# Strassen's seven products for the second experts, and maxima over partitions without GpSimd

## The chip, the cores and the metric

The kernel runs on one core of one Trainium2 chip, in one launch. Its engines work side by side, each in its own order, and wait for one another by semaphores: PE (TensorE) multiplies, DVE (VectorE), ACT (ScalarE) and POOL (GpSimd) work element by element, SP (SyncE) issues the transfers. SBUF holds tiles, PSUM what the matmuls write. The metric is the device time of one execution in microseconds, the median of several runs.

## The reference

```python
attn = softmax(q @ k^T / 8 + bias, causal window of 128) @ v      # 4 batches, 8 heads, 576 positions, 64 wide
x = attn as 2304 tokens x 512
h = np.maximum(x @ w_in, 0.0); x = h * h @ w_out                  # 512 -> 2048 -> 512
logits = x @ w_gate; P = np.exp(logits - logits.max())            # 8 experts
for _ in range(8):
    P /= P.sum(1, keepdims=True) + 1e-09
    P /= P.sum(0, keepdims=True) + 1e-09
    P *= N / E
for e in range(8):
    h = np.maximum(x @ w1[e], 0.0)                                # 512 -> 1024
    out += P[:, e:e + 1] * (h @ w2[e])                            # 1024 -> 512
```

All inputs and the output are 32-bit floats.

## The kernel before

Each number that enters a matmul is split into two 16-bit floats, a high part (HI) and the remainder (LO). A product of two split numbers is three matmuls, `PAIRS`: high by high, high by low, low by high. The high part is made by ACT (`g_hi`, `ex_hi`), the low one by DVE, which subtracts the high part from the value (`g_lo`, `ex_lo`), or by POOL in the earlier parts (`minus`, L478).

The 2304 tokens are 18 tiles of 128, in five blocks j of 4, 2, 4, 4 and 4 tiles. The program has three parts that overlap at their edges: the attention (to about 430 us), the first experts (`h_part`, `y_part`, to about 600 us), and the second experts (from 594 us to the end), which the change rewrites.

In the second experts, for each expert e, each block j and each of 8 slices f of 128 hidden columns, `g_prod` (L1480) makes 12 matmuls with the weights as the stationary operand and the block's tokens as the moving one (512 columns, 256 in block 1) into one of two PSUM banks of tag h. ACT makes the ReLU's high part from PSUM (L1493), DVE its low part (L1497), and `o_prod` (L1506) multiplies each tile of 128 tokens by w2 into four banks of tag y, adding over f. At f = 7 `o_add` (L1523) adds each tile to the output's sum with the token's gate as factor. Each expert's weights are loaded by SP in eight pieces of 1024 columns; DVE takes each piece's largest magnitude (L1443), POOL the largest over the partitions (`all_max`, L256, an all-reduce), four small DVE steps make a power of two of it, and ACT and DVE split the pieces (L1461, L1467). The routing (`softmax_all`, `sink_all`, L1605) uses the same all-reduce on POOL. A maximum in the earlier parts is made in another way: DVE spreads the 128 partition values over a diagonal (`diagonal`, L269), PE multiplies a matrix of ones by it (`sum_all`, L264), and DVE takes the maximum along the row (`row_max`, L273).

The order in which each engine does its work is fixed when the program is built. The class `Plan` holds units (an engine, an assumed cost, what comes before, which buffers it takes and frees) and plays them through in assumed time; of the units that are ready on a free engine the one with the smallest rank goes first. What comes out is one order for each engine. On the chip an engine keeps to that order: an instruction that waits holds up all behind it on its engine. `GEMM` is the rank of work between matmuls, `LEAD2` how many slices `g_prod` is ahead of `o_prod`.

Of the kernel before, what the change touches and what calls it, by code (L numbers as in the profile page):

```python
# [15 lines left out]
MAXALL = bass_isa.ReduceOp.max  # L16
ADDALL = bass_isa.ReduceOp.add
# [125 lines left out]
def kernel(  # L143
# [66 lines left out]
    zeros = const.tile([P, P], F16, name="zeros")  # L210
# [44 lines left out]
    def all_max(dst, src):  # L255
        POOL.partition_all_reduce(dst, src, channels=P, reduce_op=MAXALL)  # L256

# [9 lines left out]
    def diagonal(src):  # L267
        t = small.tile([P, P], F32, tag="diag", bufs=2, name="diag")
        DVE.tensor_scalar(out=t, in0=ident, scalar1=src, scalar2=None, op0=ALU.mult)  # L269
        return t  # L270
# [10 lines left out]
    def make_zeros():  # L281
        DVE.memset(zeros, 0.0)
        DVE.memset(ones, 1.0)

    def keep_warm():
# [4 lines left out]
        for _ in range(2):  # L290
            PE.matmul(t, lhsT=zeros, rhs=zeros, start=True, stop=True)
# [22 lines left out]
    def make_tail():  # L314
# [11 lines left out]
            h=2, r=2, sq=4, y=4, stage=4, scr=1, hp=8, wst=4,  # L326
# [29 lines left out]
    TINY = 0.08  # L356

# [461 lines left out]
    def plan_own(i, n0, z, before):  # L819
# [5 lines left out]
        mx = unit(PE, 0.3, norms_sum, i, n0, rank=z, take=["s"], after=[constants["zeros"], *ns])  # L825
# [278 lines left out]
    def plan_weights(kind, g, z):  # L1104
# [11 lines left out]
        if kind == "in":  # L1116
# [3 lines left out]
            al = unit(PE, 0.45, w_sum, kind, g, rank=z, take=["s"], after=[dg[-1], constants["zeros"]])  # L1120
# [15 lines left out]
        if kind == "out":  # L1136
# [3 lines left out]
            al = unit(PE, 0.3, w_sum, kind, g, rank=z, take=["s"], after=[ad, constants["zeros"]])  # L1140
# [154 lines left out]
    def plan_block(j):  # L1295
# [76 lines left out]
        al = unit(PE, 0.45, y_sum, j, rank=GEMM, take=["s"], after=[dg, constants["zeros"]])  # L1372
# [17 lines left out]
    NP = KE // 2  # L1390
    SB = 2 * DM * 4
    NSLOT = 2 * NP
    assert SB == KD * 2 * P * 4 and NSLOT * 2 * SB <= 64 * 1024
    late = {}
    es = const.tile([P, E, 4], F32, name="es")
    eg = const.tile([P, 1], F32, name="eg")
# [5 lines left out]
    def open_late():  # L1402
        pool = ctx.enter_context(tc.tile_pool(name="late", bufs=1, side="right"))
        late["all"] = pool.tile([P, 2 * NSLOT * SB // 4], F32, tag="late", name="late")

    def piece_at(kind, n, dt=F16):
        return late_at((kind * NSLOT + n % NSLOT) * SB, SB, dt)

    def w1_slot(e, p):

        return piece_at(0, e * NP + p).rearrange("p (a k f c) -> p a k f c", a=2, k=KD, f=2)

    def w2_slot(e, p):

        return piece_at(1, e * NP + p).rearrange("p (a f d) -> p a f d", a=2, f=2)

    staged = {}

    def stage_of(e, kind, p):

        v = staged[e, kind, p]
# [4 lines left out]
    def ex_load(e, kind, p):  # L1426
# [378 lines left out]
```

## Time and profile before

| what | before |
|---|---|
| median of 3 runs | 2106.78 us (2104.64 to 2108.39) |
| the profiled execution, its own time | 2106.07 us |
| its span, first to last instruction | 2104.3 us |
| PE busy | 2011.2 us, 96% of the span, 11324 matmuls |
| DVE busy | 867.2 us, 41%, 1700 instructions |
| ACT busy | 578.5 us, 27%, 1188 instructions |
| POOL busy | 270.3 us, 13%, 270 instructions |
| mean granted clock of TensorE | 0.985 of 2.4 GHz |

Busy time of PE counts each matmul to its modelled end, and matmuls overlap: how long one costs in a stream is the distance between the starts of two, not its duration. For DVE, ACT and POOL the duration of an instruction runs into the start of the next by a little too. The arrow in a row of groups or of the timeline names what ended the idle time before an instruction.

### The profile page before, as it was taken

Reading aid. Unit: us, or ns where it says so; the run is one execution under the profiler, and the core shown is the slowest. Engines: PE = TensorE matmul, PEld = TensorE weight load, DVE = VectorE, ACT = ScalarE, POOL = GpSimd, SP = SyncE. Lnnn points to the kernel's source line nnn. Section 1 sums busy time; section 2 is a strip of 40 time slices with the busy share of each in tenths; the row PEclk is TensorE's granted clock in tenths of the full one; section 3 lists DMA queues with packets and bytes.
Section 4 is the critical chain, followed back from the end, with each engine's and each line's share of the span. In section 5 each row is a group of like instructions: output and inputs, shape, how many; then the busy total and the mean of one; then the engine's idle time right before and its main releaser. Section 6 shows DMA issues by size and latency. Waiting matters only on the chain.

```text
span 2104.3 us, 27282 instructions
## 1 busy us (share of the span) xinstructions
PE 2011.2 (96%) x11324; PEld 1025.9 (49%) x11324; DVE 867.2 (41%) x1700; ACT 578.5 (27%) x1188; POOL 270.3 (13%) x270
## 2 busy tenths in 40 slices
PE   8777878889999999999999999999999999999999
PEld 7744654444445444444544454454445445444544
DVE  5998988762265134125213422522342152211212
ACT  5766576532232222112111211211121121111110
POOL 2566555412200000000000000000000000000000
PEclk9999999999999999999999999999999999999999
DMA  7576788520030011002001100200110010000001
GB/s 194 139 184 115 128 152 145 98 88 1 1 99 23 1 40 41 1 11 70 1 1 31 51 1 1 81 1 1 31 50 1 1 41 1 1 1 1 31 21 40
DMA packets 209228, 100.61 MB, mean 48 GB/s; under 512 B 178128, under 2 KB 194512, under 8 KB 209104
## 3 DMA queue, kind: packets, MB, share of 16 engines
q1 hardware_dynamic: 209104, 98.87, 19.9%
q8 instruction: 88, 1.44, 0.3%
q14 instruction: 36, 0.29, 0.0%
HBM read 65.03 MB, written 4.72 MB: 33 GB/s over the span
## 4 chain that ended last, share of the span: by engine, by line
PE 79%; DVE 12%; issue 3%; ACT 2%; DMA 2%; POOL 1%; SPq 0%; DVEq 0%; POOLq 0%; ACTq 0%
PE o L1506 34%; PE g L1480 34%; PE h L1193 5%; PE y L1228 4%; DVE e L584 1%; DMA stage<-in_moe_w_dram 1%; ACT e L595 1%; DVE r L1208 1%; DVE bits_out L1065 1%; DVE kc L456 0%; PE s L569 0%; DVE r L1206 0%; DVE late L1467 0%; DMA eT<-eh 0%; DVE vo L456 0%
## 5 line engine op out<-in xcount | busy, mean ns | idle before, releaser
L1480 PE MATMUL g<-y,late 128*128 128x512 f16 (+1 forms) x3840 | 799.0, 358 | 3.1 <-DVE hp L1497 3.1
L1506 PE MATMUL o<-late,hp 128*128 128x512 f16 x3456 | 797.4, 379 | 0.0
L1497 DVE SCALAR_TENSOR_TENSOR hp<-g,hp 128x512 f16<-128x512 f32 (+1 forms) x320 | 203.5, 636 | 914.3 <-ACT hp L1493 914.2
L1480 PEld LDWEIGHTS <-late 128*128 128x128 f16 x3840 | 375.5, 98 | 388.8 <-issue 4.8
L1506 PEld LDWEIGHTS <-hp 128*128 128x128 f16 x3456 | 337.9, 98 | 394.1 <-issue 0.2
L1493 ACT ACTIVATE hp<-g 128x512 f16<-128x512 f32 (+1 forms) x320 | 177.1, 554 | 1191.1 <-PE g L1480 1191.0
L1228 PE MATMUL y<-sq,w_out 128*128 128x512 f16 (+2 forms) x1056 | 213.8, 350 | 14.7 <-POOL sq L478 9.9
L1193 PE MATMUL h<-xT,w_in 128*128 128x512 f16 (+2 forms) x1056 | 212.2, 349 | 6.2 <-ACT r L1200 4.2
L256 POOL PARTITION_ALL_REDUCE ema<-em x16 | 6.0, 375 | 1114.8 <-DVE em L1443 1099.4
L1228 PEld LDWEIGHTS <-w_out 128*128 128x128 f16 x1056 | 100.5, 102 | 97.2 <-issue 20.7
L1193 PEld LDWEIGHTS <-w_in 128*128 128x128 f16 x1056 | 99.4, 101 | 90.1 <-issue 12.0
L478 POOL TENSOR_TENSOR sq<-r,sq 128x512 f16<-128x512 f32 (+2 forms) x88 | 95.7, 1087 | 207.0 <-ACT sq L1213 190.8
L1206 DVE SCALAR_TENSOR_TENSOR r<-r,unit_s 128x512 f32<-128x512 f32 (+1 forms) x64 | 50.6, 792 | 100.5 <-ACT r L1200 100.4
L1467 DVE SCALAR_TENSOR_TENSOR late<-stage,es,late 128x1024 f16<-128x1024 f32 x56 | 70.7, 1281 | 17.1 <-ACT late L1461 17.1
L1443 DVE TENSOR_REDUCE em<-stage 128x1 f32<-128x1024 f32 x56 | 68.1, 1216 | 17.8 <-DMA stage<-in_moe_w_dram 17.4
L1200 ACT ACTIVATE r<-h 128x512 f32<-128x512 f32 (+2 forms) x88 | 44.8, 510 | 102.9 <-PE h L1193 96.2
L595 ACT ACTIVATE e<-e,nmax 128x256 f32<-128x256 f32 (+1 forms) x144 | 68.0, 474 | 17.1 <-DVE nmax L584 16.7
L1461 ACT ACTIVATE late<-stage,es 128x1024 f16<-128x1024 f32 x56 | 62.7, 1141 | 33.9 <-DVE es L253 24.2
L478 POOL TENSOR_TENSOR eh<-e,eh 128x512 f16<-128x512 f32 (+1 forms) x56 | 65.6, 1174 | 32.0 <-ACT eh L463 25.7
L1213 ACT ACTIVATE sq<-r 128x512 f16<-128x512 f32 (+2 forms) x88 | 48.4, 550 | 73.2 <-DVE r L1206 43.5
L1523 DVE SCALAR_TENSOR_TENSOR acc_wc<-o,pd,acc_wc 128x512 f32<-128x512 f32 x56 | 39.9, 744 | 54.1 <-PE o L1506 54.1
L1523 DVE SCALAR_TENSOR_TENSOR acc_wd<-o,pd,acc_wd 128x512 f32<-128x512 f32 x56 | 39.8, 743 | 36.3 <-PE o L1506 36.3
(193 smaller groups left out, 1157.3 us busy)
## 6 DMA issues: line engine op xcount, KB each, us to landing
stage<-in_moe_w_dram SPq DMA_DIRECT2D x56, 512.0 KB, 3.8
st_in<-in_moe_w_in_dram SPq DMA_DIRECT2D x16, 512.0 KB, 5.0
st_out<-in_moe_w_out_dram SPq DMA_DIRECT2D x16, 512.0 KB, 5.3
raw_k<-in_k_dram SPq DMA_DIRECT2D x17, 256.0 KB, 3.9
raw_v<-in_v_dram SPq DMA_DIRECT2D x17, 256.0 KB, 4.3
raw_q<-in_q_dram SPq DMA_DIRECT2D x16, 256.0 KB, 3.6
late<-in_moe_w_dram SPq DMA_DIRECT2D x8, 512.0 KB, 7.9
out_dram<-acc_wc SPq DMA_DIRECT2D x8, 256.0 KB, 2.1
```

The lines of the kernel that those rows point to most:

```text
L478: POOL.tensor_tensor(out=dst, in0=src, in1=hi, op=ALU.subtract)
L595: ACT.activation(out=e[:, n, c0:], in_=e[:, n, c0:], func=ACTF.Exp, scale=-1.0, bias=m["nmax"][:, h : h + 1], accum_out=m["sum"][:, h : h ...
L1193: PE.matmul(hp, lhsT=w[:, a, kk, r], rhs=xT[j][:, b, kk, c], start=(kk == 0 and a == b), stop=(kk == KD - 1 and a == LO),)
L1228: PE.matmul(hold["y", d][:, c], lhsT=w[:, a, f % FPC, d * P : (d + 1) * P], rhs=sq[:, b, c], start=(first and c.start == 0 and a == b), st ...
L1443: DVE.tensor_reduce(out=late["m", e, kind][:, p : p + 1], in_=staged[e, kind, p], op=ALU.max, axis=AX.X, apply_absolute_value=True,)
L1461: ACT.activation(out=w[:, HI], in_=stage_of(e, kind, p), func=ACTF.Copy, scale=es[:, e, 2 * kind + 1 : 2 * kind + 2])
L1467: DVE.scalar_tensor_tensor(out=w[:, LO], in0=stage_of(e, kind, p), scalar=es[:, e, 2 * kind + 1 : 2 * kind + 2], in1=w[:, HI], op0=ALU.mul ...
L1480: PE.matmul(pt, lhsT=w[:, a, kk, f % 2], rhs=homes[j][:, c, kk], start=(kk == 0 and a == c), stop=(kk == KD - 1 and a == LO),)
L1493: ACT.activation(out=t[:, HI], in_=hold["g", e, j, f], func=ACTF.Relu)
L1497: DVE.scalar_tensor_tensor(out=t[:, LO], in0=hold.pop(("g", e, j, f)), scalar=0.0, in1=t[:, HI], op0=ALU.max, op1=ALU.subtract)
L1506: PE.matmul(pt, lhsT=h[:, a, t * P : (t + 1) * P], rhs=w[:, c, f % 2], start=(f == 0 and a == c), stop=(f == KE - 1 and a == LO),)
L1523: DVE.scalar_tensor_tensor(out=A, in0=pt, scalar=pd[:, e, i : i + 1], in1=A, op0=ALU.mult, op1=ALU.add)
```

## The change

It touches the second experts, the weights that they read, and every maximum or sum over partitions that POOL made.

- Each product is cut into halves both ways: the hidden slices into pairs of 128 columns, the 512 inputs into two halves, the block's tokens into two halves (256 columns, 128 in block 1). Of the eight products of halves Strassen's form (Winograd's variant) leaves seven, of sums and differences of the halves. An expert is worked in two groups g, 16 in all; a group has two pairs p.
- `g_prod` is called seven times for a pair and block, each time with 6 matmuls of 256 columns (128 in block 1). They add up in three PSUM banks X, Z and Y. ACT copies what has to be kept (`g_copy`, three times), DVE adds the banks to the copies (`g_add`, three times), ACT takes the ReLU (`g_relu`, four times) into 32-bit floats in SBUF, POOL makes the four sums that the second product needs (`g_sum`), and ACT and DVE split seven results into high and low (`g_hi`, `g_lo`, seven times each). Before, ACT and DVE had one instruction each on 512 columns for a slice.
- `o_prod` is called seven times for a pair and block, each with 6 matmuls of 256 columns (3 in block 1); they add up over the group's two pairs in three banks, and each of the seven states of a bank is added to one quarter of the block's output by `o_add`, one instruction of 256 columns for each tile of tokens (in the first two groups one for the quarter).
- The same sums of the tokens (`t_minus`, `t_hi`, `t_lo`: T1 to T4) are made once, of the weights (`ex_sums` on POOL, then a second `ex_hi` and `ex_lo`) for each pair.
- The all-reduces on POOL become `diagonal`, `sum_all` and `row_max`, or `sum_all` alone for sums.

```diff
--- before.py
+++ after.py
-        POOL.partition_all_reduce(dst, src, channels=P, reduce_op=MAXALL)
...
+        late["m", g, kind] = sum_all(P, late["m", g, kind])
...
+            POOL.tensor_tensor(out=a22, in0=a22, in1=a21, op=ALU.add)
+            yield
+            minus(a21, a11, a21)
+            yield
+            minus(a11, a22, a11)
+            yield
+            minus(a12, a12, a11)
...
+    PROD = {
+        1: ("X", lambda kk: kk, (0, 0)),
+        2: ("Z", lambda kk: 2 + kk, (1, 0)),
+        5: ("Y", lambda kk: 11 + 2 * kk, "T1"),
+        6: ("X", lambda kk: 6 + 2 * kk, "T2"),
+        7: ("X", lambda kk: 7 + 2 * kk, "T3"),
+        4: ("X", lambda kk: 4 + kk, "T4"),
+        3: ("Y", lambda kk: 10 + 2 * kk, (1, 1)),
+    }
+    def bank(b, g, j, p):
+        if (b, g, j, p) not in hold:
+            tag, bufs = ("av", 1) if b == "Z" else ("h", 2)
+            hold[b, g, j, p] = ps.tile([P, cols[j]], F32, tag=tag, bufs=bufs, name=f"{b}{g}_{j}_{p}")
+        return hold[b, g, j, p]
+    def g_prod(g, j, p, x):
+        b, row, y = PROD[x]
+        w = w1_slot(g, p)
+        pt = bank(b, g, j, p)
+        for kk in range(KH):
             for a, c in PAIRS:
+                rhs = forms[j, y][:, c, kk] if isinstance(y, str) else quarter(j, c, *y)[:, kk]
                 PE.matmul(
-                    pt, lhsT=w[:, a, kk, f % 2], rhs=homes[j][:, c, kk], start=(kk == 0 and a == c),
-                    stop=(kk == KD - 1 and a == LO),
+                    pt, lhsT=w[:, a, row(kk), :], rhs=rhs, start=(x in (1, 2, 5) and kk == 0 and a == c),
+                    stop=(x in (2, 3, 4) and kk == KH - 1 and a == LO), skip_group_check=True,
                 )
...
-    def g_hi(e, j, f):
-        t = hold["hp", e, j, f] = hp_slot(j)
-        ACT.activation(out=t[:, HI], in_=hold["g", e, j, f], func=ACTF.Relu)
-
-    def g_lo(e, j, f):
-        t = hold["hp", e, j, f]
-        DVE.scalar_tensor_tensor(
-            out=t[:, LO], in0=hold.pop(("g", e, j, f)), scalar=0.0, in1=t[:, HI], op0=ALU.max, op1=ALU.subtract
-        )
-
-    def o_prod(e, j, f, t):
-        if f == 0:
-            hold["o", e, j, t] = ps.tile([P, DM], F32, tag="y", bufs=4, name=f"o{e}_{j}_{t}")
-        pt, h, w = hold["o", e, j, t], hold["hp", e, j, f], w2_slot(e, f // 2)
-        for a, c in PAIRS:
-            PE.matmul(
-                pt, lhsT=h[:, a, t * P : (t + 1) * P], rhs=w[:, c, f % 2], start=(f == 0 and a == c),
-                stop=(f == KE - 1 and a == LO),
-            )
-
...
+    def g_copy(g, j, p, x):
+        t = hold["t", x, g, j, p] = t_slot(j)
+        ACT.activation(out=t, in_=bank("Y" if x == "c" else "X", g, j, p), func=ACTF.Copy)
+    def g_add(g, j, p, x):
+        t = hold["t", x, g, j, p]
+        DVE.tensor_tensor(out=t, in0=bank({"a": "Z", "b": "Y", "c": "X"}[x], g, j, p), in1=t, op=ALU.add)
+    def g_relu(g, j, p, x):
+        if x in "abc":
+            t = src = hold["t", x, g, j, p]
+        else:
+            t, src = t_slot(j), bank(x, g, j, p)
+            hold["t", x, g, j, p] = t
+        ACT.activation(out=t, in_=src, func=ACTF.Relu)
+    PLACE = {"A11": "a", "A12": "X", "A22": "c", "S1": "c", "S3": "b", "S2": "a", "S4": "X"}
+    def g_sum(g, j, p, name):
+        a, b, c, X = (hold.get(("t", x, g, j, p)) for x in "abcX")
+        if name == "S1":
+            POOL.tensor_tensor(out=c, in0=c, in1=b, op=ALU.add)
+        elif name == "S3":
+            minus(b, b, a)
+        elif name == "S2":
+            minus(a, c, a)
+        else:
+            minus(X, X, a)
+    def g_hi(g, j, p, name):
+        f = hold["f", name, g, j, p] = hp_slot(j)
+        ACT.activation(out=f[:, HI], in_=hold["t", PLACE[name], g, j, p], func=ACTF.Copy)
+    def g_lo(g, j, p, name):
+        f = hold["f", name, g, j, p]
+        DVE.tensor_tensor(out=f[:, LO], in0=hold["t", PLACE[name], g, j, p], in1=f[:, HI], op=ALU.subtract)
+    OUT = {
+        1: ("X", "A11", 0, (0, 0)), 2: ("Z", "A12", 1, (0, 0)), 6: ("X", "S2", 6, (0, 1)), 5: ("Y", "S1", 3, (1, 1)),
+        7: ("X", "S3", 4, (1, 1)), 3: ("Y", "S4", 2, (0, 1)), 4: ("X", "A22", 5, (1, 0)),
+    }
...
+    def o_prod(g, j, p, x):
+        b, name, row, _ = OUT[x]
+        f, w, pt = hold.pop(("f", name, g, j, p)), w2_slot(g, p), o_bank(b, g, j)
+        for t in range(half[j]):
+            for a, c in PAIRS:
+                PE.matmul(
+                    pt[:, t], lhsT=f[:, a, t * P : (t + 1) * P], rhs=w[:, c, row],
+                    start=(x in (1, 2, 5) and p == t == 0 and a == c),
+                    stop=(x in (2, 3, 4) and p == NP - 1 and t == half[j] - 1 and a == LO),
+                    skip_group_check=True,
+                )
...
+            for t in range(n):
+                DVE.scalar_tensor_tensor(
+                    out=A[:, t], in0=pt[:, t], scalar=pd[:, g, i + t : i + t + 1], in1=A[:, t], op0=ALU.mult, op1=ALU.add
+                )
...
+        p1 = prod(1, 0, [*after, *prev], ["h"])
+        p2 = prod(2, 1, [p1], ["av"])
+        p5 = prod(5, 2, [p1], ["h"])
+        a_ = copy("a", p1)
+        a = add("a", a_, p2)
+        plan.free(p2, "av", a)
+        ra = relu("a", a)
+        la = split("A11", ra)
+        p6 = prod(6, 3, [a_])
+        b_ = copy("b", p6)
+        c_ = copy("c", p5)
+        p3 = prod(3, 4, [c_])
+        b = add("b", b_, p3)
+        plan.free(p5, "h", b)
+        rb = relu("b", b)
+        p7 = prod(7, 5, [b_])
+        c = add("c", p7, c_)
+        rc = relu("c", c)
+        lc = split("A22", rc)
+        p4 = prod(4, 6, [c])
+        rX = relu("X", p4, take=["t"])
+        plan.free(p1, "h", rX)
+        lX = split("A12", rX)
+        s1 = total("S1", rb, lc)
+        l1 = split("S1", s1)
+        s3 = total("S3", s1, ra)
+        l3 = split("S3", s3)
+        s2 = total("S2", s3, la)
+        l2 = split("S2", s2)
+        s4 = total("S4", s2, lX)
+        l4 = split("S4", s4)
```

In the order that the plan gives, three places show what moves.

DVE in the second experts, before: rows of the program before, in block 4 of expert 1. g is the PSUM bank of `g_prod`, hp the split result, stage the loaded weights, em the maximum, late the split weights.

```order
L1497 SCALAR_TENSOR_TENSOR hp_7065<-g1_4_4_9394,hp_7065 128x512
L1443 TENSOR_REDUCE em_9372<-stage_7026 128x1
L1497 SCALAR_TENSOR_TENSOR hp_7065<-g1_4_5_9423,hp_7065 128x512
L1467 SCALAR_TENSOR_TENSOR late_5981<-stage_7026,es_86,late_5981 128x1024
L1497 SCALAR_TENSOR_TENSOR hp_7065<-g1_4_6_9452,hp_7065 128x512
```

DVE in the second experts, after: rows of the changed program, where group 10 ends and group 11 begins. X, Y and Z are banks of the first product, oX and oY of the second, late and x1 the 32-bit results in SBUF, hp0 and hp1 the split ones, acc the output's sum.

```order
L1651 TENSOR_TENSOR hp1_7165<-late_5885,hp1_7165 128x256
L1651 TENSOR_TENSOR hp0_7164<-late_5885,hp0_7164 128x256
L1696 SCALAR_TENSOR_TENSOR acc_wd_7474<-oY10_3_21073,pd_90,acc_wd_7474 128x256 x2
L1620 TENSOR_TENSOR x1_7133<-Y11_0_0_21142,x1_7133 128x256
L1451 TENSOR_REDUCE em_20367<-stage_7082 128x1
L1620 TENSOR_TENSOR late_5885<-X11_0_0_21101,late_5885 128x256
L266 TENSOR_REDUCE ema_21217<-em_20367 128x1
L1696 SCALAR_TENSOR_TENSOR acc_wd_7474<-oX10_3_20950,pd_90,acc_wd_7474 128x256 x2
L262 TENSOR_SCALAR diag_21229<-ident_66,ema_21217 128x128
L1651 TENSOR_TENSOR hp1_7165<-late_5885,hp1_7165 128x256
```

Between two matrix products DVE had one instruction of the chain; now adds, low parts and output sums stand in one row, and the low parts (L1651) read both their operands from SBUF, where L1497 read one from PSUM.

POOL at the end of the first experts, before: sq is the low part for `y_part`, the rows without a tile belong to the all-reduce's lines.

```order
L478 TENSOR_TENSOR sq3_4_6056<-r3_4_0_5982,sq3_4_6056 128x512
L256 ISA
L256 ISA ema_6093<-em_6051 128x4
L478 ISA
L478 TENSOR_TENSOR sq3_5_6100<-r3_5_0_6082,sq3_5_6100 128x512
```

The same place after: late are the weights of group 0, summed by `ex_sums`.

```order
L471 TENSOR_TENSOR sq3_5_6068<-r3_5_0_6014,sq3_5_6068 128x512
L1500 TENSOR_TENSOR late_5885<-late_5885 128x2x128
L471 TENSOR_TENSOR late_5885<-late_5885 128x2x128
L1500 TENSOR_TENSOR late_5885<-late_5885 128x2x128
L471 TENSOR_TENSOR late_5885<-late_5885 128x2x128 x4
L471 TENSOR_TENSOR sq3_6_6168<-r3_6_0_6152,sq3_6_6168 128x512
```

The all-reduce and the rows around it are gone; in their place seven sums of weights stand between two low parts.

POOL in the second experts had one all-reduce for each set of weights and nothing else. After: L1637 begins the four sums of a pair, the L471 behind it are the other three.

```order
L1637 TENSOR_TENSOR late_5885<-late_5885 128x256
L471 TENSOR_TENSOR late_5885<-late_5885 128x256 x3
L1637 TENSOR_TENSOR x1_7133<-x1_7133,late_5885 128x256
L471 TENSOR_TENSOR late_5885<-late_5885,x1_7133 128x256
L471 TENSOR_TENSOR x1_7133<-x1_7133 128x256 x2
L1500 TENSOR_TENSOR stage_7082<-stage_7082 128x2x128
L471 TENSOR_TENSOR stage_7082<-stage_7082 128x2x128 x3
```

The four sums of a pair follow one another, and the sums of weights stand between two pairs.

## Rows read from the trace of the kernel before

**Rows 1.** The page's chain that ended last, by engine, shares of span.

```profile
PE 79%; DVE 12%; issue 3%; ACT 2%; DMA 2%; POOL 1%; SPq 0%; DVEq 0%; POOLq 0%; ACTq 0%
```

**Rows 2.** Windows, 594:2104: us, busy of PE, PEld, DVE, ACT, POOL, clock.

```profile
594.00:2104.00 1510.00, 1502.58 (x7366) 717.98 (x7364) 456.85 (x723) 260.99 (x417) 9.55 (x24) 1.00 0.07 23
```

**Rows 3.** Groups by form, PE: names xcount | busy us, mean ns | idle.

```profile
L1506 PE MATMUL o<-late,hp 128*128 128x512 f16 x3456 | 797.4, 379 | 0.0
L1480 PE MATMUL g<-y,late 128*128 128x512 f16 x3072 | 704.7, 379 | 2.0 <-DVE hp L1497 2.0
...
L1480 PE MATMUL g<-y,late 128*128 128x256 f16 x768 | 94.3, 273 | 1.1 <-DVE hp L1497 1.1
```

**Rows 4.** Timeline of PE, 637 us: start us, us, line, operation, xcount.

```profile
637.41 1.47 PE L1480 MATMUL g<-y,late 128*128 128x256 f16 x12
638.72 2.75 PE L1506 MATMUL o<-late,hp 128*128 128x512 f16 x12
641.31 1.47 PE L1480 MATMUL g<-y,late 128*128 128x256 f16 x12
```

**Rows 5.** Timeline of PE at 74 us, products 128 columns wide.

```profile
73.93 0.83 PE L1193 MATMUL h<-xT,w_in 128*128 128x128 f16 x12
```

**Rows 6.** Timeline of all engines, 464 to 479 us, an all-reduce on POOL.

```profile
465.01 0.39 POOL L256 PARTITION_ALL_REDUCE ema<-em  x1 [5.89 <-PE h L1193]
...
472.56 2.26 POOL L478 TENSOR_TENSOR sq<-r,sq 128x512 f16<-128x512 f32 x2 [7.16 <-issue]
...
473.75 4.85 PE L1228 MATMUL y<-sq,w_out 128*128 128x512 f16 x11 [9.24 <-POOL sq L478]
```

**Rows 7.** Timeline of PE at 616 us, a maximum's product with ones.

```profile
616.90 0.38 PE L264 MATMUL total<-diag,ones 128*128 128x128 f32 x2
617.12 4.05 PE L1480 MATMUL g<-y,late 128*128 128x512 f16 x18
```

**Rows 8.** Groups by form: DVE, then POOL and ACT at 256 columns.

```profile
L1467 DVE SCALAR_TENSOR_TENSOR late<-stage,es,late 128x1024 f16<-128x1024 f32 x56 | 70.7, 1281 | 17.1 <-ACT late L1461 17.1
L1443 DVE TENSOR_REDUCE em<-stage 128x1 f32<-128x1024 f32 x56 | 68.1, 1216 | 17.8 <-DMA stage<-in_moe_w_dram 17.4
...
L1497 DVE SCALAR_TENSOR_TENSOR hp<-g,hp 128x256 f16<-128x256 f32 x64 | 27.1, 423 | 138.9 <-ACT hp L1493 138.9
...
L478 POOL TENSOR_TENSOR eh<-e,eh 128x256 f16<-128x256 f32 x12 | 9.8, 815 | 5.4 <-ACT eh L463 4.0 <-POOL eh L478 0.9 <-PE y L1228 0.4
...
L1213 ACT ACTIVATE sq<-r 128x256 f16<-128x256 f32 x20 | 8.2, 412 | 10.2 <-DVE r L1206 7.4 <-DVE r L1208 1.4 <-PE y L1228 1.4
```

**Rows 9.** Source L1206: xcount, ns min/median/max, first and last start, forms.

```profile
L1206 DVE SCALAR_TENSOR_TENSOR r<-r,unit_s x64: 467/750/1642, 196.6 to 592.1; 128x512 f32<-128x512 f32 x48, 128x256 f32<-128x256 f32 x16
```

**Rows 10.** Source L456: xcount, ns min/median/max, first and last start, forms.

```profile
L456 DVE SCALAR_TENSOR_TENSOR vo<-raw_v,sc,vo x15: 736/1140/1642, 87.2 to 380.2; 128x512 f16<-128x512 f32 x15
```

**Rows 11.** Source L653: xcount, ns min/median/max, first and last start, forms.

```profile
L653 DVE TENSOR_TENSOR x<-av,r x18: 676/690/693, 28.7 to 423.6; 128x512 f32<-128x512 f32 x18
```

**Rows 12.** Timeline at the kernel's end, two DVE instructions back to back.

```profile
2097.80 1.41 DVE L1523 SCALAR_TENSOR_TENSOR acc_wd<-o,pd,acc_wd 128x512 f32<-128x512 f32 x2 [7.10 <-PE o L1506]
```

**Rows 13.** Timeline of all engines at 361 us, DVE beside POOL.

```profile
360.67 0.74 DVE L456 SCALAR_TENSOR_TENSOR kc<-raw_k,sc,kc 128x512 f16<-128x512 f32 x1
...
361.47 1.28 POOL L478 TENSOR_TENSOR qc<-raw_q,qc 128x512 f16<-128x512 f32 x1 [0.74 <-ACT qc L463]
...
361.66 1.64 DVE L456 SCALAR_TENSOR_TENSOR vo<-raw_v,sc,vo 128x512 f16<-128x512 f32 x1
```

**Rows 14.** Windows view, 100 to 400 us, columns as in the second group.

```profile
100.00:400.00 300.00, 244.04 (x2041) 148.25 (x2041) 262.06 (x641) 193.97 (x512) 175.62 (x158) 0.94 0.74 142
```

**Rows 15.** Timeline of all engines at 1000 us, a product handed on.

```profile
1000.66 2.75 PE L1506 MATMUL o<-late,hp 128*128 128x512 f16 x12
1000.92 0.60 ACT L1493 ACTIVATE hp<-g 128x512 f16<-128x512 f32 x1 [4.58 <-PE g L1480]
1001.55 0.69 DVE L1497 SCALAR_TENSOR_TENSOR hp<-g,hp 128x512 f16<-128x512 f32 x1 [3.85 <-ACT hp L1493]
```

More of the change, by code (lines that the diff above doesn't have):

```diff
@@ L1139, in plan_weights @@
             ad = unit(DVE, TINY, w_out_add, g, rank=z, after=sq)
[L1140 removed]
+            al = unit(PE, 0.3, w_sum, kind, g, rank=z, take=["s"], after=[ad, constants["ones"]])
             us = chain(
@@ L1691, in plan_experts @@
+            if kind and g < PARTS:
+                gated[g] = unit(DVE, 0.1, first_gate, g, rank=8000, after=[scales[g, 0], sc])
+        gated = {}
         weights(0, 0)
         weights(0, 1)
+        forms_, room, room2 = plan_forms(lgt, gone[NP:])
+        early = unit(SP, 0.0, t_early, rank=-10, take=["t"] * T_EARLY, lag=0.0)
+        plan.free(early, "t", *room)
         sums = {}
+        prev = []
         first_z = LATER + 100 * KF * NB
-        for e in range(E):
-            if e == 1:
+        for g in range(NG):
+            if g == PARTS:
@@ new lines, in plan_experts @@
+                at += 100 * NP + LAG2 - LEAD2
+                last = []
+                for k_, x in enumerate(OUT):
+                    b, name, _, (r, c) = OUT[x]
+                    for p in range(NP):
+                        new = p == 0 and b not in begun
+                        last = [
+                            unit(
+                                PE, c_pe(3 * half[j], HD), o_prod, g, j, p, x, rank=at + 14 * (NP * k_ + p),
+                                take=["y"] if new else [], after=[fs[p][name][1], *ready[1][g * NP + p], read.get(b), *last],
+                            )
+                        ]
+                        if new:
+                            begun[b] = last[0]
+                        outs[p].append(last[0])
+                        plan.free(fs[p][name][0], "hp", last[0])
+                    first = (j, r, c) not in sums
+                    w = half[j] * HD
+                    eng, cost = (ACT, c_act(w, 0.1)) if first else (DVE, c_dve(w, 1.17) + (0.11 if g >= PARTS and half[j] == 2 else 0.04))
+                    u = unit(
+                        eng, cost, o_add, g, j, x, first, rank=GEMM,
+                        after=[last[0], gated[g], *ended, *sums.get((j, r, c), [])],
+                    )
+                    read[b] = u
+                    sums[j, r, c] = [u]
@@ L1744 @@
+                for b in begun:
+                    plan.free(begun[b], "y", read[b])
+                for p in range(NP):
+                    used[1][g * NP + p] = outs[p]
+                if g == NG - 1:
+                    for t in range(nt):
+                        unit(SP, 0.8, o_out, j, t, rank=GEMM, after=[*sums[j, t // half[j], 0], *sums[j, t // half[j], 1]])
+            if g + 1 < NG:
+                weights(g + 1, 0)
+                weights(g + 1, 1)
     with tc.manual_schedule():
-        u = constants["zeros"] = unit(DVE, 0.3, make_zeros, rank=-3)
+        u = constants["ones"] = unit(DVE, 0.2, make_ones, rank=-3)
```

479 lines of the change are left out of this document (303 added, 176 removed).

## The prediction

> **What bounds the kernel now.** I read the chain of waits first, then a window over the second experts, then PE's groups by form, then the timeline. The chain that ended last runs over PE for 79% of the span [rows 1]: the reader is to see that no other engine has more than 12% of it. From 594 us to the end PE is busy for 1502.6 of 1510 us, DVE for 457, ACT for 261, POOL for 10, at a granted clock of 1.00, the 2.4 GHz level [rows 2]. So this part ends when PE has done its matmuls. PE's idle time ahead of them sums to about 3 us [rows 3]. What a matmul costs in the stream comes from starts: twelve of 256 columns run from 637.41 to 638.72, 109.2 ns each, and the twelve of 512 columns behind them to 641.31, 215.8 ns each [rows 4]. Twelve of 128 columns take 0.83 us to the end of the last; a lone one lasts about 0.22, so the other eleven starts are 55.5 ns apart [rows 5].
>
> **What the change takes from PE.** Before: 6528 matmuls of 512 columns (3072 and 3456) and 768 of 256 [rows 3], 6528 x 0.2158 + 768 x 0.1092 = 1492.6 us. After, counted in the program: 5376 of 256 columns and 1344 of 128 in the first product, 6048 of 256 in the second, 11424 x 0.1092 + 1344 x 0.0555 = 1322.1 us. That is 170.5 us less, nearly the eighth that seven products of eight save; halving the columns costs almost nothing by these rows. The Trainium skill speaks against this: "TensorE: Matmul & The Clock Gate", section "Back-to-back issue gap", gives about 81 ns for each matmul of 128 columns in a stream that loads weights for each one. Rows 5 are such a stream and show 55.5. By the page the 1344 narrow ones would cost 34 us more; I keep the row.
>
> **What else leaves or comes on PE.** At 465 us POOL makes an all-reduce of 0.39 us and then does nothing for 7.16 us that the profile could put down to any wait; PE waits 9.24 us for the low part behind it, and its next eleven matmuls take 4.85 us where 2.54 would do, at the lower clock [rows 6]. With no all-reduce left this goes: 12 us with the slow start. But seven sums of weights now stand ahead of the next low part on POOL, and 33 sums for the tokens, two in three as long as POOL's 1.28 us in [rows 13] or a little less, fall in the same stretch; I count 8 us gained, with 12 and a loss of 5 as ends. The maxima come to PE: 33 products with ones at 0.22 us [rows 7] and eight narrow ones, 8 us. The old waits of 3 us go. The first pair of all has few second products to fill the waits inside it, and in the last block the second products stand alone: for these two ends no row exists; between nothing and 16 us I take 8.
>
> With PE as the only limit the span would be 2104.3 - 170.5 - 8 + 8 - 3 + 8 = 1938.8 us.
>
> **DVE, ACT and POOL for one pair.** A pair on a full block has 84 matmuls, 9.17 us of PE; there are 128 such and 32 half ones, worth 144 full ones. DVE's instructions overlap their neighbours by 0.076 us: two of 743 ns end after 1.41 [rows 12]. DVE does three adds from PSUM and seven low parts, each near 0.423 - 0.08 = 0.34 us [rows 8], and seven output sums with a factor from memory at 0.467 - 0.08 = 0.39 [rows 9]: 3.4 + 2.7 = 6.1 us. The weights of a group cost four maxima of 1.22 - 0.08 and four low parts of 1.28 - 0.08 [rows 8], four more of three quarters' size in two pieces (1.05), and two chains of small steps, taken as 0.8 each: 15.1 us on nine pairs' worth, 1.7 us. Together 7.8 of 9.17 us: 85%, where DVE had 30% [rows 2]. ACT has 14 instructions of at most 0.41 us [rows 8] and its share of the weights, no more than DVE's 1.2 us of low parts: under 7 us. POOL has four sums and 16 more for a group's weights, at most 0.82 us each [rows 8]: 3.3 + 1.5, under 5 us. None of the three is the limit by its work alone.
>
> **What the low parts wait for.** One term is missing, and the trace shows it in another stage. At 361.66 us a DVE instruction with both operands in SBUF takes 1.64 us where its twin a microsecond before takes 0.74; a POOL instruction that began at 361.47 ends at 362.75, and DVE ends 0.55 us after it [rows 13]. Of 15 such instructions the median is 1140 and the longest 1642 ns against 736 at the least [rows 10], with POOL busy for 176 of 300 us [rows 14]. An add with an operand in PSUM never passes 693 ns in the same stretch [rows 11]. So DVE stands still until POOL's instruction ends, where both its operands lie in SBUF. All seven low parts of a pair are of this kind now; before, L1497 read PSUM. The mean loss there was 0.40 us on 512 columns at a POOL share of 0.58; for POOL instructions half as long 0.2 us, up to 0.3 while POOL runs without a pause. In a pair POOL runs its four sums in a row and the low parts of the first three fall into it: 3 x 0.3, and 0.05 for each of the other four, 1.1 us. The lower end is chance meeting alone, some 0.3 us. DVE then needs 8.1 to 8.9 of 9.17 us.
>
> That alone does not pass PE, but the orders are fixed. After the seventh product PE needs DVE's add before it may start the fourth of the same pair, and in the changed order one or two units of six matmuls (0.66 us each) stand between. The handing on takes 0.26 us from PE's last start to ACT, 0.03 from ACT's end to DVE [rows 15], and the add 0.42: about 0.7 us if DVE is free. So there is 0 to 0.6 us of room, and a low part held up by POOL, or one output sum of two instructions (0.8 us), ahead of the add on DVE goes through to PE. Behind the waiting product on PE stand the next pair's products and the second products, which would be ready. I take 0.4 us of PE's time for each pair, a good third of 1.1 us, since DVE's 15% of idle time takes up the rest; bounds are 0 and the whole 1.1. 144 x 0.4 = 58 us.
>
> **The sum.** 1938.8 + 57.6 = 1996.4 us of span; the profiled execution had 1.8 us around its span (2106.07 against 2104.3), which gives 1998. The median of the runs was 0.7 us above that execution, and I leave the number at 1998.
>
> **The rivals.**
> *The waits are taken up.* DVE's idle time and the units between the products cover all of it. For it: the PSUM waits of before were covered nearly always, 3 us in 320 products [rows 3]. Against it: DVE had 70% of its time free then. The time is 1938.8 + 1.8 = 1941 us.
> *The hop decides.* Every seventh product meets a busy DVE: 0.8 us of output sum or 1.2 us of weights ahead of the add, 0.9 us lost on PE for each pair. 144 x 0.9 = 130 us, 2070 us. For it speaks the room of 0 to 0.6 us, against it that the plan puts the fourth product where it assumes the add done.
> *DVE becomes the limit, and the kernel slower.* If nearly every low part meets POOL at its worst, 0.90 us on 512 columns (1642 - 740), half of it here, six of them cost 2.7 us: DVE needs 10.5 us for a pair, 1.3 more than PE, 144 x 1.31 = 189 us, 2129 us. It decides from 1.2 us above PE's time on, 2.55 us of such waits in a pair. For it: POOL and DVE are fed by the same results one after the other, so that they meet more often than by chance, as in rows 10. Against it: POOL rests for nearly half of a pair. The Trainium skill has the rule in "SBUF — State Buffer", section "SBUF: two separate sides": whichever of the two starts first has the shared ports for its whole instruction; rows 13 agree, with the end 0.55 us after POOL's.
>
> **How the numbers follow.** Forecast (1955 to 2045 us) 0.50; waits taken up (below 1955) 0.22; the hop (2045 to 2103) 0.13; DVE the limit 0.13; a time within 0.2% of before, which is about what the measurement tells from no change, 0.02. Faster 0.85, same 0.02, slower 0.13. The range reaches from 1938, the sum with PE as the only limit and the larger gain at 465 us, to 2095, which takes in most of the hop and leaves out DVE as the limit.
>
> **What would show it.** Right: the granted clock stays at 1.00 after 600 us, starts of 256-column matmuls are 109 ns apart inside a unit, the wait of 9 us at 465 us is gone, PE's idle time in the second experts is 30 to 90 us and most of it is ahead of the first products, released by DVE's adds (L1620); L1651 has a median near 0.41 us and a long tail to about 0.8, L1620 has none. Wrong: idle ahead of the second products, released by low parts or output sums; L1651 as short at the median as at the tail; a clock below 1.00; or matmuls of 256 columns that start more than 115 ns apart.

## The result and the profile after

The changed kernel takes 2050.6 us, median of 4 runs (2041.8 to 2055.7); the kernel before took 2106.4 us in the same job. The ratio is 0.973, interval 0.970 to 0.977. The time lies in the predicted range, 53 us above the forecast; it is 6 us past the forecast's own band (1955 to 2045 us), in the band of "the hop decides". The profiled execution took 2050.96 us with a span of 2048.7.

The chain that ended last, answering to [rows 1], first line by engine, second by line:

```profile
DVE 46%; PE 35%; POOL 6%; issue 6%; ACT 4%; DMA 2%; SPq 0%; POOLq 0%; DVEq 0%; ACTq 0%
DVE hp L1651 13%; PE X L1588 9%; PE oX L1670 7%; DVE late L1490 7%; PE Y L1588 3%; PE h L1186 3%; PE y L1221 3%; DVE acc_wc L1696 3%; DVE acc_wd L1696 3%; PE oY L1670 3%; DVE em L1451 2%; PE Z L1588 2%; DVE late L1620 2%; POOL late L471 2%; PE oZ L1670 2%
```

PE had 79%; now DVE has the largest share, and in it the low parts of the hidden quarters (L1651) and of the weights (L1490). The window over the second experts, columns as in [rows 2]:

```profile
604.00:2048.00 1444.00, 1363.21 (x12908) 1207.21 (x12906) 1343.24 (x3086) 893.28 (x2471) 694.52 (x895) 1.00 0.09 26
```

DVE is busy for 93% where it had 30%, POOL for 48% where it had 1%, at the clock of before. PE is no longer without pauses, and the waits of PE in this stretch say who ends them (us in all, times, longest):

```profile
PE X L1588 <- DVE late L1620: 35.0, 43, 2.5
PE X L1588 <- DVE x L1620: 21.0, 23, 2.2
PE X L1588 <- DVE ema L266: 10.1, 13, 1.1
```

They stand ahead of products into bank X, and most end with DVE's adds. All pauses of PE in this stretch sum to 77 us, inside the 30 to 90 that the prediction named. DVE's groups by form in this stretch, answering to [rows 8] (count | busy, mean ns | idle before):

```profile
L1651 DVE TENSOR_TENSOR hp<-late,hp 128x256 f16<-128x256 f32 x539 | 295.0, 560 | 15.4 <-ACT hp L1647 13.4
L1651 DVE TENSOR_TENSOR hp<-x,hp 128x256 f16<-128x256 f32 x357 | 199.1, 564 | 8.3 <-ACT hp L1647 6.8
...
L1620 DVE TENSOR_TENSOR late<-X,late 128x256 f32<-128x256 f32 x79 | 32.5, 411 | 3.5 <-PE X L1588 3.4
```

The add, with one operand in PSUM, keeps 0.41 us; the low part, of the same width with both in SBUF, has a mean of 0.56. Of the low parts of 256 columns six in ten stay below 0.45 us, and the others reach up to 1.35, where the prediction had a tail to about 0.8 (rows of both widths together: ns at the least, median and most):

```profile
L1651 DVE TENSOR_TENSOR hp<-late,hp x673: 269/414/1350, 616.7 to 2035.2; 128x256 f16<-128x256 f32 x132, 128x128 f16<-128x128 f32 x37
L1620 DVE TENSOR_TENSOR late<-X,late x101: 275/408/425, 622.5 to 2028.4; 128x256 f32<-128x256 f32 x79, 128x128 f32<-128x128 f32 x22
```

PE's stream itself is as predicted:

```profile
604.67 0.82 PE L1588 MATMUL X<-y,late 128*128 128x256 f16 x6
605.33 0.82 PE L1588 MATMUL Z<-y,late 128*128 128x256 f16 x6
...
1003.70 0.50 PE L1588 MATMUL X<-late 128*128 128x128 f16 x6
```

Six starts of 256 columns take 0.66 us, 109 ns each, and six of 128 end after 0.50, that is 56 ns each behind the lone 0.22 [rows 5].

The second experts' part is best told by one number: its length, from the first product into X to the end of the span, less the 1322.1 us of its matmuls. Here it is 2048.7 - 604.67 - 1322.1 = 121.9 us. The prediction had 88.5 for it: 57.6 of waits, 8 of maxima, 8 of ends, and 14.9 of logits and end that before had too. The other 18.9 us of the miss (604.67 instead of 585.8) lie ahead of it.

The stall at 465 us [rows 6] is gone; from 400 to 500 us PE is busy for 99.6 of 100. But two others stand on PE in the first 600 us, both ahead of a maximum's product:

```profile
143.96 2.33 PE L1221 MATMUL y<-sq,w_out 128*128 128x512 f16 x10 [0.35 <-POOL w_out L471]
157.50 0.76 PE L257 MATMUL total<-diag,ones 128*128 128x128 f32 x2 [11.21 <-DVE nmax L577]
...
524.00 2.75 PE L1186 MATMUL h<-xT,w_in 128*128 128x512 f16 x12
534.12 0.76 PE L257 MATMUL total<-diag,ones 128*128 128x128 f32 x2 [7.37 <-DVE diag L262]
```

In the first, DVE had the diagonal ready at 146.8, but the product's bank was freed only by DVE's last read of the scores (L577), which DVE reached at 157.3. In the second, DVE reached the maxima late, since it had stood in its fixed order ahead of token forms (start, length, and idle before with its releaser):

```profile
523.50 0.69 DVE L1562 TENSOR_TENSOR late<-late 128x512 f16<-128x512 f32 x1 [7.63 <-ACT late L1558]
...
527.81 0.97 DVE L1562 TENSOR_TENSOR late<-late 128x512 f16<-128x512 f32 x1 [2.96 <-ACT late L1558]
```

And one gain was not predicted. The kernel before began with a pause on POOL of 7.84 us that no wait explains; after, the same instruction follows at once. Before, then after:

```profile
0.72 0.21 POOL L294 MEMSET ident<- 128x128 f32 x1 [0.29 <-POOLq L1790]
8.77 0.28 POOL L295 TENSOR_SCALAR_AFFINE_SELECT ident<-ident 128x128 f32<-128x128 f32 x1 [7.84 <-issue]
```

```profile
0.73 0.20 POOL L286 MEMSET ident<- 128x128 f32 x1 [0.29 <-POOLq L2095]
1.01 0.29 POOL L287 TENSOR_SCALAR_AFFINE_SELECT ident<-ident 128x128 f32<-128x128 f32 x1
```

### The profile page after: what moved, and what is told of

It reads as the page before. It is cut to its first block, busy times and chain, and to the rows that moved or that the text cites. A ratio compares the mean times of both kernels' runs of the same rounds, so it can differ in the third digit from the quotient of the medians.

```text
span 2048.7 us, 44009 instructions
## 1 busy us (share of the span) xinstructions
PE 1879.3 (92%) x16840; PEld 1519.0 (74%) x16840; DVE 1769.6 (86%) x4086; ACT 1218.0 (59%) x3258; POOL 1015.2 (50%) x1191
## 4 chain that ended last, share of the span: by engine, by line
DVE 46%; PE 35%; POOL 6%; issue 6%; ACT 4%; DMA 2%; SPq 0%; POOLq 0%; DVEq 0%; ACTq 0%
DVE hp L1651 13%; PE X L1588 9%; PE oX L1670 7%; DVE late L1490 7%; PE Y L1588 3%; PE h L1186 3%; PE y L1221 3%; DVE acc_wc L1696 3%; DVE acc_wd L1696 3%; PE oY L1670 3%; DVE em L1451 2%; PE Z L1588 2%; DVE late L1620 2%; POOL late L471 2%; PE oZ L1670 2%
## 5 line engine op out<-in xcount | busy, mean ns | idle before, releaser
L1588 PEld LDWEIGHTS <-late 128*128 128x128 f16 x6720 | 617.8, 98 | 153.2 <-issue 85.7
L1670 PEld LDWEIGHTS <-hp 128*128 128x128 f16 x6048 | 585.0, 98 | 71.1 <-issue 6.4
L1670 PE MATMUL oX<-late,hp 128*128 128x256 f16 x3456 | 468.1, 273 | 4.0 <-DVE acc_wd L1696 3.8
L1651 DVE TENSOR_TENSOR hp<-late,hp 128x256 f16<-128x256 f32 (+1 forms) x673 | 349.6, 534 | 17.1 <-ACT hp L1647 14.8
L1647 ACT ACTIVATE hp<-late 128x256 f16<-128x256 f32 (+1 forms) x673 | 256.2, 390 | 68.4 <-POOL late L471 49.7
L1588 PE MATMUL Y<-y,late 128*128 128x256 f16 (+1 forms) x1920 | 242.7, 263 | 2.5 <-ACT late L1616 1.2
L1651 DVE TENSOR_TENSOR hp<-x,hp 128x256 f16<-128x256 f32 (+1 forms) x447 | 228.2, 519 | 8.3 <-ACT hp L1647 6.8
L1670 PE MATMUL oY<-late,hp 128*128 128x256 f16 x1728 | 233.6, 273 | 0.0
L1588 PE MATMUL X<-late 128*128 128x256 f16 (+1 forms) x1728 | 205.9, 256 | 27.4 <-DVE x L1620 10.1
L1647 ACT ACTIVATE hp<-x 128x256 f16<-128x256 f32 (+1 forms) x447 | 169.9, 389 | 53.8 <-POOL x L471 43.7
L471 POOL TENSOR_TENSOR stage<-stage 128x256 f32<-128x256 f32 x210 | 169.1, 806 | 61.2 <-DVE late L1490 51.1
L471 POOL TENSOR_TENSOR sq<-r,sq 128x512 f16<-128x512 f32 (+2 forms) x88 | 97.1, 1104 | 154.0 <-ACT sq L1206 144.4
L1490 DVE SCALAR_TENSOR_TENSOR late<-stage,es,late 128x512 f16<-128x512 f32 (+2 forms) x180 | 169.8, 969 | 2.1
L1486 ACT ACTIVATE late<-stage,es 128x512 f16<-128x512 f32 (+2 forms) x180 | 134.2, 784 | 39.2 <-POOL stage L471 35.0
```

What stands on the lines that cost most here:

```text
L471: POOL.tensor_tensor(out=dst, in0=src, in1=hi, op=ALU.subtract)
L1486: ACT.activation(out=hi, in_=t, func=ACTF.Copy, scale=es[:, g, 2 * kind + 1 : 2 * kind + 2])
L1490: DVE.scalar_tensor_tensor(out=lo, in0=t, scalar=es[:, g, 2 * kind + 1 : 2 * kind + 2], in1=hi, op0=ALU.mult, op1=ALU.subtract)
L1588: PE.matmul(pt, lhsT=w[:, a, row(kk), :], rhs=rhs, start=(x in (1, 2, 5) and kk == 0 and a == c), stop=(x in (2, 3, 4) and kk == KH - 1 an ...
L1647: ACT.activation(out=f[:, HI], in_=hold["t", PLACE[name], g, j, p], func=ACTF.Copy)
L1651: DVE.tensor_tensor(out=f[:, LO], in0=hold["t", PLACE[name], g, j, p], in1=f[:, HI], op=ALU.subtract)
```

## The experiments

Unless said otherwise each is the changed kernel with one edit; times are medians. "Beyond" is the length of the second experts less 1322.1 us, and "start" their first product, both from the trace: 121.9 and 604.67 us for the changed kernel.

**No sums on POOL.** The 640 sums of hidden quarters are left out.

```diff
     def g_sum(g, j, p, name):
+        if name:
+            return
```

> The changed kernel without POOL's sums between hidden quarters (the 640 instructions S1 to S4 are left out, so the low parts read unsummed values); order of everything else as before. Theory: DVE is full in the second experts because its low parts (both operands in SBUF) stand still beside POOL. L1651 falls from a mean of 0.56 to about 0.42 us on 256 columns, DVE has some 150 us less to do, PE's 107 us of waits fall to about 40, and the time to 1970-2000 us. Rival (the hop): PE waits for the way copy, add, fourth product in a fixed order, whatever a low part lasts: L1651 shorter, time 2035-2050 us. Rival (DVE's own work): L1651 stays at 0.52 us or more, time within 10 us of 2050.

1989.6 us (1986.3 to 1990.5), 61 less than the changed kernel; beyond 61.3, start 605.29. Its low parts, in their groups by form:

```profile
L1653 DVE TENSOR_TENSOR hp<-late,hp 128x256 f16<-128x256 f32 x539 | 231.0, 441 | 20.5 <-ACT hp L1649 20.1
L1653 DVE TENSOR_TENSOR hp<-x,hp 128x256 f16<-128x256 f32 x357 | 152.2, 433 | 13.3 <-ACT hp L1649 13.0
```

The low parts are short again, DVE is busy for 1217 us instead of 1343, and half of what was beyond is gone. So POOL's sums are what lengthens them. The run takes away more than that, since ACT and DVE no longer wait for the sums either. That DVE is simply full in the changed kernel was my theory, and the next runs test it.

**One low part twice.**

```diff
+        for _ in range(2 if name == "A11" else 1):
             DVE.tensor_tensor(out=f[:, LO], in0=hold["t", PLACE[name], ...
```

> The changed kernel with one of the seven low parts of each pair (A11) made twice on DVE: 160 more instructions, 75 us of DVE at the measured lengths (128 of 0.5, 32 of 0.35 us). Theory: DVE has no room left, so nearly all of it comes out at the end: 2105-2125 us. Rival (the hop in a fixed order, DVE idle for 5%): the second one falls in DVE's pauses: 2055-2075 us.

2103.0 us (2096.7 to 2106.9), 52 more, a little under the theory's range; beyond 175.3. DVE is busy for 1409 us from the start on, 66 more, and 53 of these come out at the end.

**One low part on POOL.** A11's low part runs on POOL and is planned there.

```diff
-            lo = unit(DVE, c_dve(n), g_lo, ...
+            eng, cost = (POOL, c_pool(n) + 0.08) if name == "A11" else (DVE, c_dve(n))
+            lo = unit(eng, cost, g_lo, ...
```

> The changed kernel with one of the seven low parts of a pair (A11) made by POOL instead of DVE. DVE loses 160 instructions, some 85 us at their measured lengths; POOL has 160 of 0.5 to 0.8 us more. Theory (the time follows what DVE has to do, with its standing still beside POOL; leaving out the sums took 61 us, one low part more cost 52): 2005-2025 us, L1651 still at 0.56 us. Rival (POOL's longer share holds up the six others as much as was gained, or the sums come late): 2045-2075 us.

2055.0 us, no gain: the theory missed, and the time is the rival's. DVE has 34 us less to do (1308) where 85 were expected; the low parts left to it last 0.575 us on 256 columns instead of 0.562, with POOL busy for 55% of the stretch. Beyond is 129. So the time does not follow DVE's work alone. The order had changed: in the program, the work that stands on PE between a pair's seventh and fourth product is 1.32 us on average instead of 1.62, worked out over its 160 pairs with 2400 columns to a microsecond.

**A low part's price in the plan.** Not one instruction differs, only the order from the second experts on. The plan took a low part for 0.34 us; the trace has 0.41 alone and 0.56 beside POOL.

```diff
-            lo = unit(DVE, c_dve(n), g_lo, ...
+            lo = unit(DVE, c_dve(n) + 0.14, g_lo, ...
```

> The changed kernel with one number of the plan changed: a low part of a pair is planned 0.14 us longer, at the length that the trace shows beside POOL; the instructions are the same, in another order from the second experts on. Theory (DVE is full): the order moves little, 2035-2052 us. Rival (the order is at fault, PE's fourth and first products stand where the plan wrongly takes DVE's add for done): PE's waits fall to half, 1990-2015 us.

1993.6 us (1992.0 to 1998.4), 57 less: the rival. Beyond is 69.7. Of PE's waits these are the largest:

```profile
PE X L1588 <- DVE late L1620: 8.4, 11, 1.8
PE X L1588 <- DVE x L1620: 6.3, 6, 2.4
```

Its low parts still last 0.55 us:

```profile
L1651 DVE TENSOR_TENSOR hp<-late,hp 128x256 f16<-128x256 f32 x525 | 280.1, 549 | 9.2 <-ACT hp L1647 8.6
L1651 DVE TENSOR_TENSOR hp<-x,hp 128x256 f16<-128x256 f32 x371 | 201.1, 548 | 5.9 <-ACT hp L1647 5.4
```

DVE is busy for 1323 of 1392 us, 95%. What fell is the waiting of the two engines for each other: from the last start of the seventh product to the start of DVE's add the median is 1.01 us instead of 1.71 (in [rows 15] the next engine begins 0.26 us behind PE's last start). The plan in its own assumed time has 0.83 us there with the new price and had 0.60 with the old one. So with the old price DVE came 1.1 us later than planned, and with the new one 0.2. The work on PE between the seventh and fourth product grew too, from 1.62 to 1.73 us.

**The sums on DVE.** `g_sum` issues on DVE, planned there.

```diff
-        return unit(POOL, c_pool(n) + 0.08, g_sum, ...
+        return unit(DVE, c_dve(n), g_sum, ...
```

> The changed kernel with the sums between hidden quarters on DVE instead of POOL, planned there. DVE gets 640 instructions more, some 196 us undisturbed, and loses the standing still of about 120 us that the run without the sums showed. Theory (low parts stand still beside POOL): L1651 at 0.41-0.44 us, DVE at 97% or more, 2080-2115 us. Rival (a low part is long for another reason, as its two SBUF operands themselves): L1651 stays at 0.52 us or more, 2160 us or more.

2035.5 us (2026.6 to 2037.2), better than either side had. L1651 falls to means of 0.45 and 0.46 us with POOL busy for 231 of 1428 us, and DVE for 1401 us, 98%. Here DVE is full. The sums take 232 us on DVE, counted from each start to the next, and its busy time grows by 58 only: the low parts of the pairs alone are 135 us shorter in all.

**Short sums for the tokens.** 20 instead of 50 POOL instructions; the sums lack the low halves.

```diff
             minus(t, quarter(j, HI, *one), v)
             yield
-            POOL.tensor_tensor(out=t, in0=quarter(j, LO, *one), in1=t, op=ALU.add)
...
             minus(t, quarter(j, HI, *one), quarter(j, HI, *two))
             yield
-            minus(u, quarter(j, LO, *one), quarter(j, LO, *two))
             yield
-            POOL.tensor_tensor(out=t, in0=t, in1=u, op=ALU.add)
```

> The changed kernel with one POOL instruction instead of two or three for each of the tokens' sums (20 instead of 50 in all, the values are not the sums). Theory: the wait of 7.4 us on PE at 527-534 us comes from DVE, which stands behind low parts of token sums that POOL has not made yet; it goes, the second experts start at 596-599 instead of 604.7 us, the time is 2041-2045 us. Rival: it comes from the one bank and the one diagonal tile that all maxima share now: no change, 2048-2053 us.

2036.5 us (2030.9 to 2037.9), 14 less and more than expected; start 589.8 (runs with all the sums: 596.4 to 605.3), and from 500 to 605 us PE is busy for 104.4 us instead of 97.6 of 105. PE has no pause left from 500 us to the start. The token sums are the cause of the second stall.

**The maxima alone.** The kernel before, with its 25 all-reduces as products with ones.

```diff
-            al = unit(POOL, 0.4, ex_all, e, kind, rank=z, after=mx)
+            dg = chain(DVE, [TINY, 0.2], ex_diagonal, e, kind, rank=z, after=mx, lag=1.0)
+            al = unit(PE, 0.3, ex_all, e, kind, rank=z, take=["s"], after=dg[-1:])
```

> The kernel before, with one part of the change alone: the experts' maxima, the routing's maximum and its sums are products with ones, and nothing is an all-reduce on POOL. Theory: the wait of 9.24 us at 465 us and its slow start go and nothing else moves, 10 to 12 us less than before, 2093-2097 us. Rival: the products wait for DVE's diagonals and PE's stream is cut 20 to 30 times instead: 2102-2110 us.

2086.1 us, 19.6 less than before (ratio 0.991, 0.990 to 0.993), better than either side expected. PE's busy time from 0 to 100 us rises from 80.5 to 88.5 us and from 400 to 500 from 90.1 to 100.0: both pauses of POOL are gone, the one at the start too. Start 571.73.

**The first memset's price.** The change had replaced a memset planned at 0.3 us by one planned at 0.2. This puts the number back.

```diff
-        u = constants["ones"] = unit(DVE, 0.2, make_ones, rank=-3)
+        u = constants["ones"] = unit(DVE, 0.3, make_ones, rank=-3)
```

> The changed kernel with one number of the plan changed: the first memset is planned with 0.3 us, as in the kernel before, instead of 0.2; no instruction is another, but the order up to the logits is that of the kernel before. Theory: the 11.2 us for which PE stands at 146-157 us ahead of a total come from the other order alone, and go; the second experts start at 588-594 instead of 604.7 us, the time is 2032-2042 us. Rival (the attention part is slower for the granted clock or for the one diagonal tile, not the order): 2046-2055 us.

2034.4 us (2033.6 to 2035.5), 16 less, as the theory had it; start 589.23. With 0.3 the order on PE is that of before, row by row, up to the logits; with 0.2 it parts from it after the attention's first 18 units on PE. Six runs with 0.2 and an unchanged first part start their second experts at 596.4 to 605.3 us, mean 600.2, three with 0.3 at 588.6 to 589.2: 11.2 us apart. That this is also the length of the first stall is chance, since the stall does not go: the same product now waits 6.98 us, for another step of DVE, as it waited 6.61 us in the kernel before.

```profile
153.18 0.80 PE L257 MATMUL total<-diag,ones 128*128 128x128 f32 x2 [6.98 <-DVE diag L262]
```

The rest is other waits, and the clock: from 250 to 300 us the granted clock is 0.73 in all six with 0.2, and 0.86 to 0.90 in those with 0.3 and in the kernel before. Which waits are worth how much was not taken apart.

**Both numbers of the plan.**

> The changed kernel with the two numbers of the plan together: low parts of a pair 0.14 us dearer, the first memset at 0.3 us. Theory (two separate losses, 57 us in the second experts' order and 16 us in the attention part's): they add up, 1973-1983 us. Rival (the early gain is taken back later, since DVE is the limit behind it): 1988-1996 us.

1980.1 us (1978.2 to 1981.5): the gains add up, start 588.64, beyond 69.0. In the second experts the order on PE is that of the run with the low part's price alone, which had 69.7, as the run with the memset's price alone has the changed kernel's and 122.0 where that had 121.9. So the same order gives the same length within 1 us.

**All prices.** Both numbers, and these:

```diff
-        return chain(POOL, [c_pool(KH * cols[j])] * n, t_minus, ...)[-1]
+        return chain(POOL, [c_pool(KH * cols[j]) + 0.3] * n, t_minus, ..., lag=SLOW)[-1]
...
-        us = [unit(DVE, c_dve(n1, 1.17), ex_lo, ...
+        us = [unit(DVE, c_dve(n1, 1.17) + 0.3, ex_lo, ...
-        us.append(unit(DVE, c_dve(W, 1.17), ex_lo, ...
+        us.append(unit(DVE, c_dve(W, 1.17) + 0.2, ex_lo, ...
```

> As the one with two numbers, and the other work that meets POOL is planned at the length that the trace shows: the weights' low parts 0.3 and 0.2 us dearer, a POOL instruction of the tokens' sums 0.3 us dearer, and their result counted as there 1 us later. Theory (what is planned too short comes late, and the engine behind it stands): the wait of 7.4 us at 527-534 us goes and some of the waits in the second experts, 1958-1972 us. Rival (what is left is DVE's own work): 1973-1983 us as without it.

1996.2 us: a miss for both. Start 578.58, ten earlier, but beyond 94.1.

**More than the measured price.** Both numbers, with 0.24 for 0.14.

> As the one with two numbers, with the low parts 0.24 instead of 0.14 us dearer in the plan, more than they last in the trace. Theory (the price is right where it meets the trace): no better, 1973-1990 us. Rival (any slack ahead of PE's fourth product helps further): 1955-1970 us.

2131.4 us, slower than before: neither. Beyond 218.5, clock 0.95 in this stretch. The waits, now for ACT's copies, first of PE, then of ACT:

```profile
PE Y L1588 <- ACT x L1616: 62.1, 15, 8.5
PE Y L1588 <- ACT late L1616: 36.1, 10, 8.5
```

```profile
ACT late L1486 <- POOL stage L471: 86.4, 54, 3.2
```

ACT stands ahead of the weights' high parts (L1486), and the copies that PE needs are queued behind. By its own numbers the plan then has DVE at some 9.4 us for a pair, above PE's 9.2 (three adds, seven low parts at 0.576, 3.5 output sums at 0.78, a ninth of the weights' 15 us). The loss is in the plan already: in its own assumed time DVE has 1402 us of work in this part where it has 1290 with 0.14, and the part ends 153 us later; on the chip it is 150 us longer. Why the plan loses more than DVE's 1402 us ask for was not tried.

**Both numbers and the tokens' price.**

> As the one with two numbers, and of the further prices only the tokens' sums' (0.3 us dearer, counted as there 1 us later), the weights' low parts at their old price. Theory (the run with all prices gained 10 us before the second experts by the tokens' sums and lost 25 behind it by the weights' price): second experts start at 577-581 us, 1966-1973 us. Rival (any other order in the second experts is luck, and this one is another again): 1978-2000 us.

1969.9 us (1967.2 to 1971.9, 5 runs), ratio 0.935 to before (0.934 to 0.937), the fastest of all: start 578.59, beyond 68.6.

## Why the prediction was right or wrong

*The matmuls, right.* The starts are 109 and 56 ns apart as worked out, the clock stays at 1.00, and 1322 us stand under every version. The 81 ns for 128 columns that the Trainium skill gives ("TensorE: Matmul & The Clock Gate", section "Back-to-back issue gap") is not seen after either.

*The all-reduce, half seen.* I read the pause behind it, 9.2 us, and not its twin at the kernel's start, which was in the same trace. With the other waits that the run of the maxima alone took away they are worth 19.6 us, where I had 12. The Trainium skill has such a pause in "GPSIMD Engine Reference", section "2.1 Instruction dispatch": a first call of freshly loaded code costs about 6 us without an instruction in the profile. Here the two were 7.84 and 7.16 us. That code is loaded in them no run shows, and the first of them stands 440 us ahead of the first all-reduce; shown is that both go when no all-reduce is left.

*What takes it back, mis-sized.* I set the new sums on POOL at 4 us against the 12 of the stall. By the start of the second experts they cost 10 us (their price in the plan, 578.6 for 588.6) and by the time 14 (20 instructions for 50). Another 11 us went by a line of the diff that I passed over, the planned 0.2 us of a memset: it changes no work, but it re-orders the whole attention part. So the second experts began 10.9 us later than before in the profile where I had 8 us earlier. Not all of it is found: with both put right they begin at 578.6 us, with the maxima alone at 571.7, and the single diagonal tile, of which the change leaves one of two, was not tried apart.

*The low parts beside POOL, right in kind and nearly in size.* Taking the sums away shortens L1651 by 0.12 to 0.13 us on 896 instructions, 111 us, and all of DVE by 126 us: 0.8 to 0.9 us a pair, where I had 1.1. The Trainium skill's rule on the shared ports in "SBUF — State Buffer", section "SBUF: two separate sides", takes in a DVE instruction with two inputs in SBUF, and the trace agrees: L1620, with an operand in PSUM, stays at 0.41 us.

*What of it reaches PE, mis-sized: the step that failed.* I let DVE's 15% of idle time take up all but 0.4 us of 1.1. With the other terms as forecast, the measured 121.9 - 88.5 + 57.6 = 91 us are 0.63 us a pair instead of 0.4. Of such idle time hardly any was left: DVE's busy time is 1343 / 144 = 9.3 us a pair, above my 8.1 to 8.9 and, with the routing in it, above PE's 9.17. And its order was made for less, since the plan took a low part for 0.34 us and had 1134 us of work for DVE in this part. So the adds came on DVE behind more work than the plan reckoned with, 1.1 us late at the median, and PE met them late. With the trace's length as price, the same instructions, with low parts still at 0.55 us, lose 52 us less.

*The rivals.* "The hop decides" had the right place, bank X behind DVE's adds, and 0.63 us lies midway between my 0.4 and its 0.9. But the waits are not the fourth product's alone: of PE's pauses, worked out from the starts (98 us, against 77 by the modelled ends), 43 us lie ahead of first products and 38 us ahead of fourth ones. DVE was full only where the sums were put on it, and even there the kernel was faster than before. But it was near to being the limit: its 1343 us are more than PE's 1322, and in the better order its 1323 us are as many, so that below some 1320 us for this part both have to do less.

*What stays open.* That a price near the measured length gives the best order is not shown. With 0.1 us more the kernel is slower than before, and with the weights' low parts at their length too the second experts take 25 us longer, of which the plan's own time has 10. The order decides, and one order gives one length; what makes one good is shown for these prices alone.

## What to carry to other kernels

Where a planner fixes the order, compare its price for each instruction with the duration in the trace under the new neighbours: here one planned 0.14 us too short made its engine late, and the engine behind it waited, for 52 us in all. Read the end of the plan in its own time as well, since the slowest order had its loss there before it ran. Read the diff for planned numbers as for instructions, since 0.1 us on a memset moved the second experts by 11 us. And count a slow kind of instruction by all the pauses that vanish when the program has none left, not by the one behind it.

## What was not expected of the hardware

A program with all-reduces on POOL had a pause of 7.84 us near its start, 440 us before the first of them at 449.5 us; two programs without any (the changed kernel and the one with the maxima alone) do not have it, though POOL's queue holds the same configuring instruction there, at 0.9 us. A low part of 256 columns lasts 0.56 us with POOL busy for 48% of the stretch, and 0.43 to 0.46 with 16%, in the two programs without the sums on POOL. Of the 896 low parts of 256 columns in the changed kernel, 375 began while a POOL instruction ran and outlasted it; their end lies 0.28 us behind POOL's at the median. The other 521 last 0.43 us at most, so that all of the lengthening is of this kind. At 512 columns, in the attention of the kernel before (L456), the end lies 0.55 us behind POOL's.
